# A planned instruction order: ties to VectorE, engines of early pieces as a list, the verdict before the last down projection

## The chip, the cores and the metric

The kernel runs on one core of one Trainium2 chip. The metric is the time of one execution in microseconds (us). TensorE multiplies matrices, VectorE, ScalarE and GpSimd work on tiles, SP issues all transfers.

## The reference

A linear attention with decay over 768 steps, for 4 batches and 8 heads of 48 features, and behind it a feed-forward layer with the maximum of three projections. Cut to what is computed:

```
for t in range(S):                       # 768 steps, per batch and head
    cur = outer(u * k[t], v[t])
    y[t] = r[t] @ (state + cur)
    state = w * state + outer(k[t], v[t])
x = y over all heads                     # 3072 tokens x 384
h = max(x @ w1, x @ w2, x @ w3)          # 3072 x 768
out = h @ w_out                          # 3072 x 384
```

## The kernel before, in words

The 768 steps are cut into 12 chunks c of 64 steps (`NCH`, `C`); a chunk holds 256 tokens (4 batches). Heads go in two halves q of four. For each (c, q) the features of k and r are scaled by powers of the decay (`scale`, line 526), TensorE forms scores, a mask keeps what lies before the diagonal (line 628), the bonus u comes onto the diagonal, and TensorE forms the values from the scores and the carried state (`values`, line 661). The state is brought forward by one product per chunk (`keys`, `into_state`, line 649).

Numbers are split in a high and a low fp16 part, and three of the four products are taken. In chunks 0 and 1 (`FULL`) the attention runs in fp32 instead; there the state is spread into its operand by `state_apart` (line 676), four ScalarE instructions, and the bonus comes as a product pp of the scaled k and r (`joined`, line 561), a matmul `bonus` with it (line 569), and a predicated copy. From `EARLY` on the bonus is formed from the token layout.

`ffn(c)` (line 1090) takes six blocks f of the hidden layer. For each, three up projections go into accumulators of a ring of four (`psm`, line 720); the first becomes m by `first` on ScalarE (line 735), the other two by `least` on VectorE, a maximum (line 739). ScalarE makes the high part hh (line 742), GpSimd or VectorE the low part hl (`lows_by` and `h_low`, lines 744 to 748). Three down projections m = 0, 1, 2 then leave through ScalarE (line 765) and SP (line 1128). The weights come as 64-bit words in 16 pieces of 576 KB; each piece takes ScalarE (line 377), VectorE (line 381), ScalarE (line 384) and VectorE again (line 388) to split.

The fast path is exact only while the inputs lie in ranges. So sums of squares are taken on the way (lines 392, 514), `check_ends` (line 778) and `check` (line 782) test them on VectorE, `count` (line 794) adds up the good rows on TensorE, `verdict` (line 798) makes a flag, and `flagged` (line 804) loads it into a register of every engine. Line 1180 branches on it: with a flag of 0 the general path behind it is jumped over.

What sets the order: every engine's queue is written out by a planner. `do` (line 166) records a piece of work with a due number, engine, cost, what it reads and writes, and the buffers that it takes. The due number grows with the chunk, and `SHIFT` adds a number by engine, kind and one of four stages. `order` (line 190) then lists the pieces one by one: among those that could start first by the planner's clock it takes the lowest due number. `near` marks pieces of VectorE and GpSimd that read two operands from SBUF; the planner doesn't let one of each engine overlap. When a VectorE piece of that kind is about to be listed and a GpSimd one could start as early, both compete by their due numbers. The listed order is emitted at lines 1175 to 1177, each queue runs it strictly in turn, and semaphores hold what isn't ready.

Of the kernel before, what the change touches and what calls it, by code (L numbers as in the profile page):

```python
# [1 line left out]

# [18 lines left out]
C = 64  # L21
# [5 lines left out]
U = 8  # L27
# [44 lines left out]
class Plan:  # L72

    LAG = {"pe": 0.22, "dve": 0.12, "act": 0.15, "pool": 0.12, "sp": 0}
    FREE = dict(pe=5.1, dve=4.4, act=4.0, pool=10.5, sp=2.1)
    SLACK = dict(pe=0.022, dve=0, act=0, pool=0, sp=0.324)
    LANES, BEFORE, BEHIND = 8, 1.1, 0.9
    PHASE, PIPE, STIR = -0.626, 3.4, 1.1
    RATE = {"feat": 300e3, "tok": 280e3, "word": 325e3, "again": 280e3, "u": 300e3, "kb": 200e3, "ktb": 235e3, "sb": 265e3, "vb": 255e3, "io": 300e3, "vl": 240e3, "x4": 150e3}
    STAGES = (-0.01, 1.6, 4.2)  # L80
    SHIFT = {
        "act ah": (-51.918, -65.498, -45.263, -70.501),
        "act eye16": (2.479, 10.868, 2.479, 2.479),
        "act hh": (-33.526, -14.287, -83.034, -18.026),
        "act his": (-38.269, -57.533, -17.347, -17.347),
        "act io": (-20.889, -66.792, 14.503, -29.26),
        "act kdh": (-43.057, -58.602, -10.774, -29.53),
        "act kt": (-30.9, -10.226, 7.514, 7.514),
        "act ktdh": (-3.857, 40.692, 1.455, 33.711),
        "act ktdl": (3.565, -0.867, 3.565, 3.565),  # L90
        "act m": (-70.203, -41.092, -60.922, -75.724),
        "act rh": (19.916, 12.704, 32.612, 53.416),
        "act sb": (0.145, -0.176, -10.989, -10.989),
        "act sdh": (-16.606, -58.921, 1.393, -19.385),
        "act sq": (-1.212, -23.443, 14.89, -12.959),
        "act state": (33.684, 26.281, 28.467, 28.467),
        "act tkf": (-17.604, -31.369, -17.604, -17.604),
        "act tkt": (22.733, 36.039, 22.733, 22.733),
        "act u": (4.631, 27.167, 4.631, 4.631),
        "act vdh": (-17.326, -39.923, -45.144, -6.375),  # L100
        "act wsq": (10.215, 10.215, 10.215, -8.248),
        "act xh": (30.286, 24.252, -17.669, -20.556),
        "act xsq": (-6.009, -27.049, 24.787, 11.067),
        "act ztop": (-4.699, -20.204, 10.624, 10.624),
        "dve a": (26.38, 26.38, 11.139, -1.961),
        "dve al": (17.989, 15.173, 12.796, 3.439),
        "dve am": (55.107, 70.564, 45.761, 45.639),
        "dve ama": (30.643, 9.956, 13.112, 13.112),
        "dve ends": (12.35, 12.35, 12.35, -28.973),
        "dve flag": (1.454, 1.454, 1.454, -27.608),  # L110
        "dve good": (-5.938, -5.938, -5.938, -17.176),
        "dve hl": (-37.322, -78.745, -108.013, -56.219),
        "dve kT": (-16.831, -12.831, -12.831, -12.831),
        "dve kdl": (0.885, -7.723, -39.713, -26.204),
        "dve ktdl": (-5.025, -5.025, -36.996, 18.823),
        "dve lo": (-0.26, -6.619, 7.806, 7.806),
        "dve m": (-20.646, -47.146, 3.792, -49.546),
        "dve pp": (9.143, -7.503, -7.503, -7.503),
        "dve rT": (10.984, 17.021, 17.021, 17.021),
        "dve rl": (-7.775, 1.143, 7.87, 0.054),  # L120
        "dve sdl": (10.363, 27.381, 7.967, -24.341),
        "dve state": (-21.286, 12.093, -11.87, 12.772),
        "dve uw": (0.32, 1.8, 1.8, 1.8),
        "dve vdl": (-17.961, -18.008, 30.606, -24.481),
        "dve wc": (-6.358, 8.855, 8.855, 8.855),
        "dve word": (-0.926, 1.508, 3.967, 3.967),
        "dve xl": (-27.474, -19.943, -51.504, -89.07),
        "pe bo": (-52.734, 1.414, 10.831, 10.831),
        "pe count": (3.343, 3.343, 3.343, 38.72),
        "pe dn": (-0.067, -15.416, -14.654, -0.182),  # L130
        "pe ke": (-0.01, -23.579, -0.382, 0.04),
        "pe kea": (-7.875, 12.914, 2.838, 2.838),
        "pe read": (4.637, 4.637, 4.637, 18.248),
        "pe sc": (-0.084, -31.697, -0.512, -0.419),
        "pe sca": (-3.935, 71.214, 12.28, 12.28),
        "pe th": (-9.587, -62.178, -9.587, -9.587),
        "pe tha": (23.917, 65.739, 34.635, 34.635),
        "pe turned": (-13.591, 14.048, -13.591, -13.591),
        "pe up": (-0.117, -7.456, -0.433, -0.157),
        "pe va": (-0.206, 16.327, -15.548, -0.297),  # L140
        "pe vaa": (-12.853, -16.75, -19.32, -19.32),
        "pool am": (-17.715, -17.715, -5.033, -19.033),
        "pool hl": (-48.799, -21.273, -76.69, -49.446),
        "pool kT": (34.361, 53.386, 38.392, 59.601),
        "pool kdec": (-10.665, -10.665, 19.908, 1.651),
        "pool pp": (27.125, 25.693, 41.112, 41.112),
        "pool rT": (43.765, 63.373, 35.752, -3.803),
        "sp again": (8.471, 8.471, 8.471, 55.836),
        "sp feat": (-52.564, 4.808, 0.643, 1.927),
        "sp first": (-13.276, -15.501, -15.501, -15.501),  # L150
        "sp io": (14.829, -21.632, 41.797, 39.859),
        "sp kb": (-2.952, -16.917, 3.534, 14.738),
        "sp ktb": (17.782, -6.916, 9.699, 12.373),
        "sp sb": (-23.628, -37.745, -29.113, 17.159),
        "sp tok": (-33.778, 55.686, -34.574, -42.289),
        "sp u": (-34.129, -15.755, -34.129, -34.129),
        "sp vb": (7.415, 6.46, 39.433, -0.198),
        "sp vl": (-12.349, 18.562, 18.562, 18.562),
        "sp word": (-15.193, 28.55, -3.374, -3.374),
# [6 lines left out]
    def do(self, due, eng, cost, fn, reads=(), writes=(), takes=(), size=0, near=0, n=1, active=1.0, kind=None):  # L166
# [4 lines left out]
        name = eng + " " + what  # L171
# [15 lines left out]
        self.todo.append(dict(n=k, due=due, due0=due0, stage=stage, eng=eng, cost=cost, fn=fn, need=need, takes=takes, size=size, near=near, nd=n, active=active, kind=name,  # L187
                              rate=self.RATE[what] if size else 0, touch={*reads, *writes, *new}))

    def order(self):  # L190
# [16 lines left out]
        def earliest(p):  # L207
# [1032 lines left out]
```

## Time and profile before

| | |
|---|---|
| runs, us | 385.55, 385.65, 388.21; median 385.65 |
| the profiled execution | 389.68 us, span 387.9 us |
| TensorE matmul busy | 372.6 us, 96% of the span, 5039 |
| VectorE busy | 252.4 us, 65%, 519 |
| ScalarE busy | 256.5 us, 66%, 673 |
| GpSimd busy | 185.3 us, 48%, 194 |
| DMA | 78.28 MB, mean 202 GB/s |
[...]

Times in the rows count from the start of the span. PE is TensorE, PEld its weight loads, DVE VectorE, ACT ScalarE, POOL GpSimd; a q behind the name is the engine's sequencer, which also handles semaphores, register loads and branches. A busy time holds a wait for operands that begins after an instruction has started. Idle time is given with what ended it. [...]

### The profile page before, as it was taken

The numbers are of one execution on the slowest core, as the hardware profiler recorded it, in microseconds if no ns is written. First come the engines' busy times: TensorE is split into PE (matmuls) and PEld (weight loads), VectorE is DVE, ScalarE is ACT, GpSimd is POOL, SyncE is SP. The second block draws the span as 40 slices with busy tenths as digits, with TensorE's granted clock in tenths as the row PEclk, the third lists the DMA queues.
The fourth block names the chain that finished last, engine by engine and source line by source line (L and its number), as shares of the span: only waits on it lengthen the run. The fifth ranks groups of instructions, "written<-read, shape, count | busy, mean of one in ns | idle before, by whom it ended". The sixth has DMA issues, their size and how long they took to land.

```text
span 387.9 us, 12500 instructions
## 1 busy us (share of the span) xinstructions
PE 372.6 (96%) x5039; PEld 333.3 (86%) x5039; DVE 252.4 (65%) x519; ACT 256.5 (66%) x673; POOL 185.3 (48%) x194
## 2 busy tenths in 40 slices
PE   8978999999999999979999999999999999999993
PEld 5857888999999999959999999999999989999883
DVE  6678999958586675967585585485586385352530
ACT  2968788576856846736766766666766787994421
POOL 9561442555855853844735745745745614020210
PEclk9989999999999999989999999999999999999997
DMA  7994499689966996972886886886896885930001
GB/s 195 377 294 147 131 349 275 190 234 248 298 164 189 269 252 181 286 222 80 226 226 177 245 227 170 253 228 159 265 229 179 238 233 139 284 119 29 16 0 48
DMA packets 32320, 78.28 MB, mean 202 GB/s; under 512 B 8576, under 2 KB 13824, under 8 KB 32256
## 3 DMA queue, kind: packets, MB, share of 16 engines
q1 hardware_dynamic: 32256, 77.42, 69.8%
q8 instruction: 41, 0.67, 0.7%
q14 instruction: 23, 0.19, 0.2%
HBM read 37.59 MB, written 4.72 MB: 109 GB/s over the span
## 4 chain that ended last, share of the span: by engine, by line
PE 69%; DMA 12%; DVE 5%; ACT 4%; issue 3%; POOL 3%; SPq 2%; DVEq 0%; ACTq 0%; POOLq 0%
PE psm L720 56%; DMA tok<-in_tok_dram 8%; PE psa L674 6%; PE psa L614 4%; DMA feat<-in_feat_dram 2%; ACT junk L514 1%; DMA kb<-kd 1%; DMA sb<-sd 1%; DVE m L739 1%; DVE sd L694 1%; PE psa L575 1%; PE psa L586 1%; POOL pp L564 1%; ACT kd L498 1%; DVE xl L715 1%
## 5 line engine op out<-in xcount | busy, mean ns | idle before, releaser
L720 PEld LDWEIGHTS <-w 128*128 128x128 f16 x2592 | 250.2, 98 | 34.0 <-issue 4.6
L720 PE MATMUL psm<-xh,w 128*128 128x256 f16 x1296 | 222.3, 274 | 3.2 <-DVE m L739 3.2
L720 PE MATMUL psm<-xl,w 128*128 128x256 f16 x648 | 154.7, 274 | 0.0
L739 DVE SCALAR_TENSOR_TENSOR m<-psm,m 128x256 f32<-128x256 f32 x144 | 60.4, 421 | 65.3 <-PE psm L720 43.1
L748 POOL TENSOR_TENSOR hl<-m,hh 128x256 f16<-128x256 f32 x55 | 39.3, 715 | 98.7 <-ACT hh L742 94.1
L529 POOL TENSOR_TENSOR feat<-feat,wrt 128x512 f32<-128x512 f32 x44 | 58.0, 1327 | 31.3 <-DMA feat<-in_feat_dram 31.3
L720 PE MATMUL psm<-hh,w 128*128 128x256 f16 x432 | 56.0, 273 | 0.0
L742 ACT CAST hh<-m 128x256 f16<-128x256 f32 x72 | 28.5, 398 | 36.3 <-DVE m L739 36.0
L514 ACT ACTIVATE junk<-tok 128x384 bf16<-128x384 f32 x72 | 37.5, 521 | 18.1 <-DMA tok<-in_tok_dram 17.2
L548 POOL TENSOR_TENSOR am<-tok,u_sb 128x384 f32<-128x384 f32 x18 | 19.6, 1087 | 54.7 <-DVE al L638 44.3
L715 DVE SCALAR_TENSOR_TENSOR xl<-psa,xh 32x256 f16<-32x256 f32 (+2 forms) x60 | 28.3, 472 | 16.2 <-ACT xh L710 15.4
L735 ACT ACTIVATE m<-psm 128x256 f32<-128x256 f32 x72 | 27.2, 377 | 10.4 <-PE psm L720 9.2
L720 PE MATMUL psm<-hl,w 128*128 128x256 f16 x216 | 33.4, 273 | 0.0
L710 ACT ACTIVATE xh<-psa 32x256 f16<-32x256 f32 (+2 forms) x60 | 24.9, 415 | 9.3 <-PE psa L674 8.9
L674 PE MATMUL psa<-rh,sb 128*128 128x64 f16 x320 | 29.5, 193 | 0.0
L674 PE MATMUL psa<-ah,vb 128*128 128x64 f16 x320 | 29.5, 193 | 0.0
L674 PE MATMUL psa<-rl,sb 128*128 128x64 f16 x160 | 28.4, 193 | 0.0
L674 PE MATMUL psa<-al,vb 128*128 128x64 f16 x160 | 28.4, 193 | 0.0
L765 ACT ACTIVATE io<-psm 128x256 f32<-128x256 f32 x36 | 13.0, 374 | 21.5 <-PE psm L720 21.4
L674 PEld LDWEIGHTS <-vb 128*128 128x128 f16 x480 | 26.3, 98 | 0.4
L674 PEld LDWEIGHTS <-sb 128*128 128x128 f16 x480 | 25.0, 98 | 0.0
L503 DVE TENSOR_TENSOR kd<-feat,kd 128x512 f16<-128x512 f32 x20 | 19.0, 952 | 4.4 <-ACT kd L498 4.3
(107 smaller groups left out, 546.8 us busy)
## 6 DMA issues: line engine op xcount, KB each, us to landing
tok<-in_tok_dram SPq DMA_DIRECT2D x24, 576.0 KB, 6.8
feat<-in_feat_dram SPq DMA_DIRECT2D x22, 512.0 KB, 5.2
raw<-in_ws_dram SPq DMA_DIRECT2D x12, 576.0 KB, 6.8
kb<-kd SPq DMA_DIRECT2D x20, 256.0 KB, 5.4
kb<-kd SPq DMA_DIRECT2D x20, 248.0 KB, 5.5
ktb<-ktd SPq DMA_DIRECT2D x18, 256.0 KB, 7.2
out_dram<-io SPq DMA_DIRECT2D x36, 128.0 KB, 4.9
ktb<-ktd SPq DMA_DIRECT2D x18, 248.0 KB, 7.5
```

The costliest lines, as they stand in the source:

```text
L503: nc.vector.tensor_tensor(out=dense.dense[:, 1, :, 0:w], in0=src, in1=dense.dense[:, 0, :, 0:w], op=ALU.subtract)
L514: nc.scalar.activation(out=junk[:, 0:U * D].rearrange("p (u d) -> p u d", u=U), in_=src, func=AF.Square, scale=scale, accum_out=stat[:, ki ...
L529: (nc.gpsimd if c else nc.vector).tensor_tensor(out=t[n], in0=t[n], in1=tb, op=ALU.mult)
L548: helper(c).tensor_tensor(out=w.rearrange("p (g b) d -> p g b d", g=2), in0=t["r"], in1=by_token(u_sb, q), op=ALU.mult)
L674: nc.tensor.matmul(out=t["va"][0:n, i, :], lhsT=a, rhs=b, start=k == 0, stop=k == len(prods) - 1)
L710: nc.scalar.mul(out=hi, in_=src, mul=x_scale(c))
L715: nc.vector.scalar_tensor_tensor(out=lo, in0=src, scalar=x_scale(c), in1=hi, op0=ALU.mult, op1=ALU.subtract)
L720: nc.tensor.matmul(out=ps, lhsT=a, rhs=b, start=first and n == 0, stop=last and n == len(prods) - 1)
L735: nc.scalar.mul(out=m, in_=ps, mul=by)
L739: nc.vector.scalar_tensor_tensor(out=m, in0=ps, scalar=by, in1=m, op0=ALU.mult, op1=ALU.max)
L742: nc.scalar.copy(out=h[0][:, f, :], in_=m)
L748: lows_by(c, f).tensor_tensor(out=h[1][:, f, :], in0=m, in1=h[0][:, f, :], op=ALU.subtract)
```

## The change

*The planner.* All numbers of `SHIFT` are new (a few are shown), as are `FREE` (when each engine is first free) and `SLACK` (how far a piece may be put off for one with a lower due number). A `near` piece of GpSimd is taken to start `SEIZE` = 0.33 us later. In a tie it is now the GpSimd piece that can be displaced, by any VectorE piece that could start as early. Costs of some pieces are longer.

*Engines.* `flex` records a piece with several engines, and `CHOICE` names, by the piece's number in the order of recording, which of them is taken; a piece without an entry takes the first. The first engine of the list is VectorE for scaling (chunks 0 to 3), pp and, in chunks 0 and 1, hl; it is ScalarE for m, the first state and its spread.

*The checks.* The check of the ends moves from due 4.9 to 10, behind the start of chunk 9 instead of chunk 4. The check of the sums, the count, the flag and its load are recorded before `ffn` of the last chunk, and its last down projection (m = 2) now reads "read", so that it is listed behind the load. The last sum of squares of x and the repeated sums of the weights fall due earlier. The conditional general path stays at the end.

```diff
-    FREE = dict(pe=5.1, dve=4.4, act=4.0, pool=10.5, sp=2.1)
-    SLACK = dict(pe=0.022, dve=0, act=0, pool=0, sp=0.324)
+    FREE = dict(pe=5.15, dve=4.2, act=4.2, pool=10.5, sp=2.36)
+    SLACK = dict(pe=0, dve=0.059, act=0.146, pool=0.589, sp=0.419)
+    SEIZE = 0.33
...
+    CHOICE = {30: 1, 31: 2, 47: 1, 134: 1, 135: 1, 137: 1, 152: 1, 153: 1, 178: 1, 186: 1, 188: 1, 196: 1, 202: 1, 212: 1, 234: 1, 235: 1, 241: 1, 264: 1, 265: 1, 296: 1, 302: 1, 310: 1, 312: 1, 318: 1, 320: 1, 326: 1, 334: 1, 336: 1, 342: 1, 359: 1, 391: 1, 392: 1}
     SHIFT = {
...
-        "dve word": (-0.926, 1.508, 3.967, 3.967),
+        "dve word": (88.415, 131.798, 76.497, 30.189),
-        "pe up": (-0.117, -7.456, -0.433, -0.157),
+        "pe up": (-44.638, -143.074, -77.684, -76.534),
-        "pe read": (4.637, 4.637, 4.637, 18.248),
+        "pe read": (0, 0, 0, -80.672),
-        "sp feat": (-52.564, 4.808, 0.643, 1.927),
+        "sp feat": (-27.4, -40.095, 30.336, -8.959),
-        "sp vl": (-12.349, 18.562, 18.562, 18.562),
+        "sp vl": (-17.172, -10.657, -10.657, -0.468),
-        "sp word": (-15.193, 28.55, -3.374, -3.374),
+        "sp word": (68.802, 88.992, 63.732, 36.065),
...
+        if alts:
+            eng, cost, near = (base, *alts)[self.CHOICE.get(k, 0)]
+            fn = partial(fn, eng)
...
             elif p["eng"] == "pool" and p["near"]:
+                t += self.SEIZE
...
-            if e == "dve" and self.todo[n]["near"]:
-                rival = [m for m in when if self.todo[m]["eng"] == "pool" and self.todo[m]["near"] and when[m] <= when[n] + 1e-6]
+            if e == "pool" and self.todo[n]["near"]:
+                rival = [m for m in when if self.todo[m]["eng"] == "dve" and when[m] <= when[n] + 1e-6]
...
-    def state_apart(q):
-        for g in range(2):
-            j = 2 * q + g
-            for hh in range(2):
-                w = sb[q].wide[HS[hh], g * B:(g + 1) * B, hh * D:(hh + 1) * D]
-                nc.scalar.mul(out=w, in_=state[HS[hh], j], mul=wc[HS[hh], j:j + 1])
+    def state_apart(q, e):
+        for hh in range(2):
+            if e != "act":
+                w = sb[q].wide[HS[hh], :, hh * D:(hh + 1) * D].rearrange("p (g b) d -> p g b d", g=2)
+                by = wc[HS[hh], 2 * q:2 * q + 2].unsqueeze(2).unsqueeze(3).broadcast_to([C, 2, B, D])
+                by_name[e].tensor_tensor(out=w, in0=state[HS[hh], 2 * q:2 * q + 2], in1=by, op=ALU.mult)
+                continue
+            for g in range(2):
+                j = 2 * q + g
+                nc.scalar.mul(out=sb[q].wide[HS[hh], g * B:(g + 1) * B, hh * D:(hh + 1) * D], in_=state[HS[hh], j], mul=wc[HS[hh], j:j + 1])
 
...
+    def flex(due, options, fn, **on):
+        fn = fn if len(options) > 1 else partial(fn, options[0][0])
+        do(due, *options[0][:2], fn, near=options[0][2], alts=options[1:], **on)
...
+        options = [("dve", dve(U * C), 1), ("pool", 1.27, 1)] if c < 4 else [("pool", 1.27, 1)]
...
+            flex(due - 0.32 + 0.02 * i, options, lambda e, n=n: scale(c, q, n, e), reads=reads, writes=[(n, c, q)])
+            flex(due - 0.16, [("dve", dve(U * C), 1), ("pool", 1.27, 1)], lambda e: joined(c, q, e), reads=[f, ("kT", c, q), ("rT", c, q)], takes=[("pp", ("pp", c, q))])
+            flex(due + 0.02, [("act", act(U * D), 0), ("dve", 0.5, 0)], lambda e: into_state(c, q, e), reads=[("ke", c, q)], writes=[s])
+            flex(due + 0.06, [("act", 1.85, 0), ("pool", 2.1, 1), ("dve", 0.95, 1)], lambda e: state_apart(q, e), reads=[s, "wc"], writes=[("sb", q)])
...
+                    flex(due - 0.2, [("act", act(TOK), 0), ("dve", dve(TOK), 0)][:2 if c < 2 else 1], lambda e, f=f: do_tile(("m", c, f), first(T["up", c, f, 0], TOK, H16, e)), reads=[("up", c, f, 0)], writes=[] if f else [("begun", c)], takes=[("m", ("m", c, f))])
+            options = [("dve", dve(TOK), 1), ("pool", 0.73, 1)]
+            if c > 1:
+                options = options[1:] if f < NF - 1 else options[:1]
+            flex(due - 0.1, options, lo, reads=[m, ("hh", c, f), *([("hl", c)] if f else [])], writes=[("hl", c, f)], takes=[] if f else [("hl", ("hl", c))])
...
+            reads = (["read"] if c == NCH - 1 and m == NM - 1 else []) + [k for a in ("hh", "hl") for k in ((a, c), *((a, c, f) for f in fs))] + [(a, *n) for n in w for a in ("his", "lo")]
...
-        ffn(c)
+            ffn(c)
     for n in range(NW):
         for h in range(2):
-            again(n, h, NCH - 2.6 + 0.25 * n + 0.12 * h)
+            again(n, h, NCH - 2.8 + 0.22 * n + 0.11 * h)
     for i in range(2 * EARLY):
         squares_again(i // 2, i % 2, NCH - 3 + 0.25 * i)
-    do(4.9, "dve", 1.2, check_ends, reads=[("begun", 4)], writes=["ends"])
-    do(NCH - 0.4, "dve", 1.5, check, reads=["ends", *(k for k in plan.wrote if k[0] in ("sq", "xsq", "wsq"))], writes=["good"])
-    do(NCH - 0.35, "pe", 0.1, count, reads=["good"], takes=[("psa", "count")])
-    do(NCH - 0.35, "dve", 0.1, verdict, reads=["count"], writes=["flag"])
-    do(NCH - 0.16, "pe", 0.1, flagged, reads=["flag"], writes=["read"])
+    do(NCH - 2, "dve", 2.4, check_ends, reads=[("begun", NCH - 3)], writes=["ends"])
+    do(NCH - 1 + 0.45, "dve", 2.4, check, reads=["ends", *(k for k in plan.wrote if k[0] in ("sq", "xsq", "wsq"))], writes=["good"])
+    do(NCH - 1 + 0.5, "pe", 0.1, count, reads=["good"], takes=[("psa", "count")])
+    do(NCH - 1 + 0.5, "dve", 0.15, verdict, reads=["count"], writes=["flag"])
+    do(NCH - 1 + 0.55, "pe", 0.1, flagged, reads=["flag"], writes=["read"])
+    ffn(NCH - 1)
```

## Rows read from the trace of the kernel before

**Rows 1.** Stretch, length; busy (x) of PE, PEld, DVE, ACT, POOL; granted clock, DMA.

```profile
28.00:76.00 48.00, 46.56 (x603) 40.95 (x602) 44.32 (x76) 38.02 (x81) 17.78 (x15) 1.00 0.70 213
200.00:250.00 50.00, 50.00 (x710) 45.78 (x708) 29.21 (x62) 32.04 (x88) 31.20 (x32) 1.00 0.79 220
300.00:340.00 40.00, 39.36 (x540) 35.78 (x538) 21.58 (x48) 33.23 (x97) 13.11 (x14) 1.00 0.80 226
```

**Rows 2.** TensorE's waits over the span: us in total, times, longest.

```profile
PE psm L720 <- DVE m L739: 3.2, 2, 2.5
PE psa L575 <- POOL pp L564: 2.6, 1, 2.6
PE psa L674 <- issue: 1.3, 1, 1.3
```

**Rows 3.** Busy time and granted clock in the stretches behind TensorE's waits.

```profile
22.00:24.00 2.00, 1.32 (x6) 0.76 (x8) 2.00 (x3) 1.20 (x3) 0.63 (x1) 0.54 1.02 229
24.00:26.00 2.00, 2.00 (x13) 1.10 (x10) 0.58 (x1) 0.00 (x0) 0.01 (x1) 0.60 0.97 323
168.00:170.00 2.00, 2.00 (x14) 1.62 (x14) 1.95 (x5) 1.35 (x3) 0.38 (x1) 0.73 0.97 227
170.00:172.00 2.00, 2.00 (x12) 1.39 (x11) 0.29 (x1) 1.17 (x4) 1.92 (x3) 0.50 1.02 399
```

**Rows 4.** GpSimd in order of time: start us, us, what.

```profile
18.95 3.68 POOL L564 TENSOR_TENSOR pp<-feat 128x512 f32<-128x512 f32 x1
...
162.00 2.92 POOL L529 TENSOR_TENSOR feat<-feat,wrt 128x512 f32<-128x512 f32 x2
```

**Rows 5.** VectorE in order of time, near two of TensorE's waits.

```profile
31.55 0.73 DVE L628 COPY_PREDICATED am<-cs,psa 128x512 f32<-128x512 int32 x1
...
151.80 0.74 DVE L694 SCALAR_TENSOR_TENSOR sd<-state,wc,sd 128x192 f16<-128x192 f32 x2
...
154.47 0.16 DVE L772 TENSOR_SCALAR bt<-wu_sb 128x4 f32<-128x4 f32 x1
...
156.77 0.16 DVE L774 TENSOR_TENSOR ends<-ends,bt 128x4 f32<-128x4 f32 x1
...
162.38 2.77 DVE L694 SCALAR_TENSOR_TENSOR sd<-state,wc,sd 128x192 f16<-128x192 f32 x2
```

**Rows 6.** Instructions by line and shape: count, busy us, mean ns, idle before.

```profile
L739 DVE SCALAR_TENSOR_TENSOR m<-psm,m 128x256 f32<-128x256 f32 x144 | 60.4, 421 | 65.3 <-PE psm L720 43.1 <-ACT m L735 14.7 <-ACT kd L498 3.2
...
L748 POOL TENSOR_TENSOR hl<-m,hh 128x256 f16<-128x256 f32 x55 | 39.3, 715 | 98.7 <-ACT hh L742 94.1 <-DVE am L628 2.5 <-DMA out_dram<-io 1.8
...
L564 POOL TENSOR_TENSOR pp<-feat 128x512 f32<-128x512 f32 x4 | 7.9, 1975 | 0.3
...
L681 ACT ACTIVATE sb<-state,wc 64x192 f32<-64x192 f32 x8 | 3.6, 452 | 0.2
...
L564 DVE TENSOR_TENSOR pp<-feat 128x512 f32<-128x512 f32 x2 | 1.4, 692 | 0.1
```

**Rows 7.** The end in order of time: ScalarE's last copy, SP's last transfer.

```profile
381.70 0.38 ACT L765 ACTIVATE io<-psm 128x256 f32<-128x256 f32 x1 [1.58 <-PE psm L720]
...
382.60 0.34 SPq L1128 DMA_DIRECT2D out_dram<-io  x1
```

**Rows 8.** Lines 805, 1180, 1235: duration ns least, median, longest; first and last start.

```profile
L805 ACTq TENSOR_LOAD <-flag x1: 463/463/463, 382.0 to 382.0; - x1
L805 PEldq TENSOR_LOAD <-flag x1: 491/491/491, 382.0 to 382.0; - x1
...
L1180 PEldq COMPARE_BRANCH  x1: 4198/4198/4198, 382.6 to 382.6; - x1
...
L1235 SPq EVENT_SEMAPHORE  x14: 17/28/567, 385.8 to 387.9; - x14
```

**Rows 9.** DMA issues from 370 us on: KB each, us to landing.

```profile
out_dram<-io SPq DMA_DIRECT2D x3, 128.0 KB, 1.8
```

**Rows 10.** VectorE near the end: the check's last instruction.

```profile
364.40 0.28 DVE L792 TENSOR_REDUCE good<-ok 128x1 f32<-128x125 f32 x1
```

More of the change, by code (lines that the diff above doesn't have):

```diff
@@ L1 @@
 from contextlib import ExitStack
+from functools import partial
 import concourse.bass as bass
@@ L86 @@
[L86 to L125, printed above, removed]
@@ new lines @@
+        "dve ama": (-67.852, -74.779, -10.739, 0.799),
+        "dve ends": (0, 0, 0, -22.298),
+        "dve flag": (0, 0, 0, 58.918),
+        "dve good": (0, 0, 0, -31.946),
+        "dve hl": (23.491, -32.082, -106.608, -65.147),
+        "dve kT": (-85.346, -11.836, 20.754, -9.76),
+        "dve kdl": (22.717, 51.739, -58.583, 17.126),
+        "dve ktdl": (-31.022, -31.022, -11.392, -41.137),
+        "dve lo": (-1.191, 40.138, -21.062, -19.786),
+        "dve m": (-101.783, -139.093, 24.699, 46.278),
@@ L164, in __init__, with do @@
         self.bufs, self.todo, self.wrote, self.read, self.turn = bufs, [], {}, {}, {}
-    def do(self, due, eng, cost, fn, reads=(), writes=(), takes=(), size=0, near=0, n=1, active=1.0, kind=None):
+    def do(self, due, eng, cost, fn, reads=(), writes=(), takes=(), size=0, near=0, n=1, active=1.0, kind=None, alts=()):
         k = len(self.todo)
@@ L170, in do @@
         what = kind or (made if isinstance(made, str) else made[0])
-        name = eng + " " + what
+        name, base = eng + " " + what, (eng, cost, near)
+        if alts:
+            eng, cost, near = (base, *alts)[self.CHOICE.get(k, 0)]
+            fn = partial(fn, eng)
         stage = sum(due > s for s in self.STAGES)
@@ L186, in do @@
         need.discard(k)
-        self.todo.append(dict(n=k, due=due, due0=due0, stage=stage, eng=eng, cost=cost, fn=fn, need=need, takes=takes, size=size, near=near, nd=n, active=active, kind=name,
+        self.todo.append(dict(n=k, base=base, alts=alts, due=due, due0=due0, stage=stage, eng=eng, cost=cost, fn=fn, need=need, takes=takes, size=size, near=near, nd=n, active=active, kind=name,
                               rate=self.RATE[what] if size else 0, touch={*reads, *writes, *new}))
@@ L647, in keys, with into_state @@
             three(t["ke"][:, i, :], [ktb.on[s][i] for s in range(2)], [vd[q].dense[:, s, i, 0:D] for s in range(2)], True, True)
-    def into_state(c, q):
+    def into_state(c, q, e="dve"):
         ps = raws[c, q].pop("ke")
         if c == 0:
-            nc.scalar.copy(out=units(state[:, 2 * q:2 * q + 2]), in_=ps)
+            (nc.scalar.copy if e == "act" else nc.vector.tensor_copy)(out=units(state[:, 2 * q:2 * q + 2]), in_=ps)
             return
@@ L731, in up, with first @@
         return ps
-    def first(ps, n, by):
+    def first(ps, n, by, e):
         m = tmp.tile([P, n], F32, name="m", bufs=3)
-        nc.scalar.mul(out=m, in_=ps, mul=by)
+        if e == "act":
+            nc.scalar.mul(out=m, in_=ps, mul=by)
+        else:
+            nc.vector.tensor_scalar(out=m, in0=ps, scalar1=by, scalar2=None, op0=ALU.mult)
         return m
@@ L908 @@
     do_tile = T.__setitem__
+    by_name = dict(dve=nc.vector, pool=nc.gpsimd, act=nc.scalar)
+    def flex(due, options, fn, **on):
+        fn = fn if len(options) > 1 else partial(fn, options[0][0])
+        do(due, *options[0][:2], fn, near=options[0][2], alts=options[1:], **on)
     def dma(due, fn, size, n=1, **on):
-        do(due, "sp", 0.42 * n, fn, size=size, n=n, **on)
+        do(due, "sp", (0.64 if on.get("kind") == "vl" else 0.42) * n, fn, size=size, n=n, **on)
     def helping(c, columns):
@@ L959, in scaled @@
     def scaled(c, q, due):
[L960 removed]
+        options = [("dve", dve(U * C), 1), ("pool", 1.27, 1)] if c < 4 else [("pool", 1.27, 1)]
         f = ("feat", c, q)
[L962 to L963 removed]
+        for i, (n, reads) in enumerate((("kT", [f]), ("rT", [f, ("rraw", c, q)]))):
+            flex(due - 0.32 + 0.02 * i, options, lambda e, n=n: scale(c, q, n, e), reads=reads, writes=[(n, c, q)])
     def before_scores(c, q, due):
@@ L975, in before_mask @@
         if c < EARLY:
-            do(due - 0.16, *(("pool", 1.28) if c else ("dve", dve(U * C))), lambda: joined(c, q), reads=[f, ("kT", c, q), ("rT", c, q)], takes=[("pp", ("pp", c, q))], near=int(c > 0))
+            flex(due - 0.16, [("dve", dve(U * C), 1), ("pool", 1.27, 1)], lambda e: joined(c, q, e), reads=[f, ("kT", c, q), ("rT", c, q)], takes=[("pp", ("pp", c, q))])
             do(due - 0.12, "pe", 0.9, lambda: bonus(c, q), reads=[("pp", c, q), "uw"], takes=[("psa", ("bo", c, q))])
```

125 lines of the change are left out of this document (71 added, 54 removed).

## The prediction

> **What bounds the kernel now.** I read the busy time by stage first, then the waits of TensorE, then the clock in the stretches behind its waits, then VectorE and GpSimd in those stretches, last the chain behind the last matmul.
>
> By stage, TensorE is busy all 50.00 us of 200 to 250 us, at full clock [rows 1]. There no reordering can gain: the work is the same before and after. VectorE is the engine to watch early: 44.32 of 48.00 us between 28 and 76 us, against 29.21 of 50.00 and 21.58 of 40.00 us in the two later stretches [rows 1].
>
> TensorE's waits are few [rows 2]: 2.6 us for the product pp, 1.3 us put down to issue, and 3.2 us in two waits for m (2.5 and so 0.7 us). Behind the long ones the clock falls to its lower level. From 22 to 24 us the granted clock is 0.54 over 1.32 us of matmul, from 24 to 26 us 0.60 over 2.00 us, which costs 1.32 x 0.46 + 2.00 x 0.40 = 1.4 us. From 168 to 172 us it costs 2.00 x 0.27 + 2.00 x 0.50 = 1.5 us [rows 3]. So there are **early holes** of 2.6 + 1.3 + 1.4 = 5.3 us and a **middle hole** of 2.5 + 1.5 = 4.0 us.
>
> Each has its cause. pp of 128x512 took 3.68 us on GpSimd from 18.95 us [rows 4], against 0.69 us of the same form on VectorE [rows 6]. VectorE was running weight conversions meanwhile, and pp came last. The wait of 1.3 us ends with the mask, which VectorE did at 31.55 us for 0.73 us [rows 5]: the values matmul that follows it starts at once. The middle hole begins where the check of the ends takes VectorE from 154.47 to 156.93 us, six instructions on 4 columns [rows 5]. Then two state instructions, 2.77 us for a pair, stand beside 2.92 us of scaling on GpSimd from 162.00 us [rows 4, 5], and m is late.
>
> **The sum's base.** The profiled execution took 389.68 us, 387.90 of them span and 1.78 around it. The runs shown have a median of 385.65, 4.03 less, just about the middle hole. I read this as: the hole belongs to some executions and not to the median one. So the sum goes 389.68 - 4.0 (middle hole) = 385.7, and from there.
>
> **The change, part by part.**
>
> 1. *Order.* Every due time is shifted anew, GpSimd's shared operations are listed 0.33 us later, VectorE wins a tie, some costs are longer. This adds no instruction and removes none, so it is worth only what it does to holes: at best +5.3 us for the early ones, all closed. At worst it makes others; no row shows the new order, so the lower end is one more hole of the middle kind, -4.0. I take **3.0**. The wait for pp needs other work in TensorE's order, or an earlier pp. At half the pair of scalings of the same form, 1.46 us [rows 4], pp would end at 20.4 instead of 22.6 us, so 2.2 of its 2.6 us and, with a hole that short, the 1.4 us of clock are to be had: 3.6. The wait of 1.3 us may stay or go, half is 0.65. Against these 4.25 I set 1.25 for a new small hole of the second kind, since VectorE gets fuller (next). On SP the new shifts still rank the first features and values before the weight words, so the first transfers keep their order; what the later ones do has no row and lies within the two ends.
>
> 2. *Engines chosen.* Counting the calls in the order in which they are listed, the 32 numbers come out so. To VectorE: seven first maxima m from ScalarE (three of chunk 0, four of chunk 1), pp of (1,1) and (2,1) and the scaling of k in (3,0) from GpSimd, the first state of pair half 0 and its spread into sb, now two instructions instead of four. To GpSimd: four low parts hl (f = 0, 1, 3 of chunk 0 and f = 5 of chunk 1), and sb of half 1, in two instructions. Everything else flexible stays where it was. For VectorE that is 7 x 0.42 = 2.9 us of m, 3 x 0.69 = 2.1 of products and scaling, less 4 x 0.42 of hl, about as one m [rows 6]: +3.3 us, most of it between 28 and 76 us, where it has 48.00 - 44.32 = 3.7 us idle [rows 1]. The state and its spread lie before that; two instructions of 0.5 to 0.7 us each by the nearest VectorE rows and one copy, +1.9. ScalarE loses 8 x 0.452 = 3.6 us of sb [rows 6]. GpSimd gains 4 x 0.715 = 2.9 us of hl and loses two pp and a scaling at 1.46 to 1.98 us [rows 4, 6]: nearly even. On the path I cost this at **0**, covered by the 3.7 us idle; if that cover is gone, m is late next, and with it the ring of four accumulators that TensorE fills.
>
> 3. *Check of the ends*, from about chunk 5 to chunk 10: 2.46 us of VectorE [rows 5] go to a stretch with 40.00 - 21.58 idle [rows 1]. **0** there. In the middle it takes away one of the two causes of that hole, already in the base.
>
> 4. *Verdict earlier.* Now the count of the good rows, the flag and its load into a register lie behind the last matmul. The last copy starts at 381.70 us [rows 7], TensorE's load of the flag at 382.0 for 0.49 us, its branch at 382.6, and the branch takes 4.2 us, to 386.8; the last semaphore is at 387.9 [rows 8]. With the load taken earlier, the branch can start as the last matmul is issued: 382.6 - 381.7 = 0.9 us earlier. More, if the sequencer runs ahead of the matmuls; then the end is set by the output instead: copy 0.38 us [rows 7], issue 0.34 [rows 7], landing 1.8 [rows 9], and 387.9 - 386.8 = 1.1 of closing barriers give 381.70 + 3.6 = 385.3, which is 2.6 earlier. The other end: the load stands in all five queues at the place of the read, TensorE pays up to 0.49 us between matmuls, VectorE's last m and hl, ScalarE's copies and SP's output transfers queue behind theirs, and 0.9 - 0.5 = 0.4 is left. I take **1.2**, nearer to the lower pair of rows. The verdict must be in hand by then: the check's last instruction ran at 364.40 us [rows 10], 17 us before the end, and its input, the last sum of squares of x, is listed earlier; **0**.
>
> [...] No row here shows how far the sequencer runs ahead.
>
> Sum: 385.7 - 3.0 - 1.2 = 381.5, against the median 385.65 - 4.2 = 381.45. I say **381.4**.
>
> **The rivals.**
>
> *A, the holes only move.* The new order closes the wait for pp and opens waits of the same size elsewhere before 80 us; the tail is all that stays: 385.65 - 1.2 = 384.4. For it: the order is made from listed costs, and in the trace the same form takes 0.69 alone, 1.98 us on GpSimd in the mean and 3.68 at worst [rows 4, 6], so small errors decide. Against it: the two costliest waits have a named cause that other work can fill.
>
> *B, slower: VectorE becomes the bound between 28 and 76 us.* Its 3.7 us idle shrink to 0.4 by the 3.3 us of part 2. From then on each instruction that has to wait for GpSimd comes straight out of TensorE: the state pair took 0.74 us at 151.80 us and 2.77 us at 162.38 us [rows 5], 2.0 us of it waiting. Two such collisions make 4.0 us, less 0.4, and each hole of that kind has its fall of the clock, 1.5 us: 3.6 + 3.0 = 6.6. With the tail's 1.2 and without the early gain 385.65 + 6.6 - 1.2 = 391.1. It decides from the point at which VectorE has no idle slice between 28 and 76 us. For it: 92% busy there now. Against it: three products leave GpSimd, so there is less to collide with.
>
> *C, the branch under the last matmuls.* The sequencer reaches the branch while matmuls still run, the output sets the end: 381.4 - 1.4 = 380.0. For it: ScalarE's load of the flag stands at the same 382.0 us although its copy runs until 382.08 [rows 7, 8]. [...]
>
> *D, the verdict is late or the read blocks the queues*, so TensorE stands before the last down projection: the load's 0.5 us, and up to 1.2 us for the rest of the tail's gain: 381.4 + 1.7 = 383.1. Against it: 17 us of slack.
>
> **How the numbers follow.** Chances: forecast 0.46, A 0.24, B 0.14, C 0.10, D 0.06. The forecast's own range is 379.3 to 383.5: 3.0 give or take 1.5 and the tail from 0.6 to 1.8. The range on record goes down to C with the early holes closed further, 378.5, and up past A with a further 2.1 us of new holes, 386.5; B lies outside. Faster by over 1%, what a measurement of this kernel can tell from no change, is under 381.8: 0.6 of the forecast (0.28), nearly all of C (0.10), a quarter of A and D (0.07), in sum 0.45. Slower is over 389.5: most of B, 0.13. The rest is 0.42.
>
> **What would show it.** Right: no wait of TensorE for pp over 1 us, no granted clock under 0.9 between 16 and 32 us, no TensorE idle near 164 us; the load of the flag stands before the last down projection and the branch at most 0.2 us after the last matmul. A: as much idle time of TensorE before 80 us as now, behind other releasers. B: VectorE over 47 of 48 us between 28 and 76 us, and m as releaser of TensorE's waits there. C: a branch that starts before the last matmul ends. D: a wait of TensorE on the flag. I am wrong if the waits close and the time stays, or if the branch takes much more or less than 4.2 us.

## The result, and the profile after

In the first comparison, four executions of each, the kernel took **381.71 us** after the change (379.99 to 381.82) and 386.53 before: ratio 0.986, 95% interval 0.981 to 0.991. Run again later beside other kernels (twelve executions, 35 of before) it took 382.21 against 385.97: ratio 0.992, 0.988 to 0.995. Ratios leave out slow executions, medians and spreads hold them all. So it is 0.8% to 1.4% faster, 3.2 to 5.4 us. The profiled execution after took 381.82 us, 380.3 of them span.

By stage, with the columns of [rows 1]:

```profile
22.00:24.00 2.00, 1.55 (x15) 1.28 (x14) 1.97 (x4) 2.00 (x5) 1.24 (x2) 1.00 1.03 337
24.00:26.00 2.00, 2.00 (x23) 1.88 (x21) 1.96 (x5) 2.00 (x5) 0.00 (x0) 1.00 1.17 256
28.00:76.00 48.00, 45.90 (x566) 40.40 (x564) 46.09 (x83) 32.46 (x70) 24.05 (x18) 1.00 0.69 218
150.00:200.00 50.00, 50.00 (x692) 45.64 (x691) 36.79 (x67) 31.15 (x88) 35.68 (x32) 1.00 0.76 214
200.00:250.00 50.00, 49.84 (x675) 45.40 (x672) 41.69 (x73) 34.13 (x93) 32.47 (x30) 1.00 0.86 227
```

The granted clock, as a share of the full one, is 1.00 where it was 0.54 and 0.60 [rows 3], and TensorE has no idle time from 150 to 200 us: the middle hole is gone. But from 28 to 76 us TensorE works 45.90 us where it worked 46.56 [rows 1], and VectorE has 1.9 us idle where it had 3.7. TensorE's waits (us in total, times, longest), answering to [rows 2]; "issue" is a wait that nothing in the profile explains:

```profile
PE psm L728 <- ACT m L744: 1.7, 1, 1.7
PE psa L590 <- issue: 1.0, 1, 1.0
PE psm L728 <- DVE m L750: 0.8, 2, 0.6
...
PE psa L579 <- DVE pp L571: 0.2, 1, 0.2
```

The wait for pp fell from 2.6 to 0.2 us; a wait of 1.7 us for ScalarE's m is new. Its cause is on VectorE and ScalarE, in order of time:

```profile
23.83 0.74 DVE L388 SCALAR_TENSOR_TENSOR raw<-raw,ztop 128x576 int32<-128x576 int32 x1
...
28.38 1.82 DVE L388 SCALAR_TENSOR_TENSOR raw<-raw,ztop 128x576 int32<-128x576 int32 x1
```
```profile
30.23 0.73 ACT L391 ACTIVATE w<-raw 128x576 f16<-128x576 f32 x1 [2.76 <-DVE raw L388]
30.87 1.52 ACT L718 ACTIVATE xh<-psa 96x256 f16<-96x256 f32 x4
32.41 0.84 ACT L384 CAST ztop<-raw 128x576 f16<-128x576 bf16 x1
33.27 0.38 ACT L744 ACTIVATE m<-psm 128x256 f32<-128x256 f32 x1
```

VectorE's word (L388 here), a step of splitting a weight piece, took 0.74 us at 23.83 and 1.82 at 28.38, beside GpSimd's scaling (26.33 to 29.58 us); ScalarE stood 2.76 us for it, and the m that TensorE wanted came three pieces later in ScalarE's queue.

The end, answering to [rows 7, 8]: the start of TensorE's first down projection of the last piece, its last down projection, ScalarE's last copy, and then the lines of the load (L813), the branch (L1197) and the closing semaphores (L1252), each with its least, median and longest ns and its starts:

```profile
371.12 1.26 PE L728 MATMUL psm<-hh,w 128*128 128x256 f16 x10
...
375.06 1.47 PE L728 MATMUL psm<-hh,w 128*128 128x256 f16 x12
376.37 0.82 PE L728 MATMUL psm<-hl,w 128*128 128x256 f16 x6
```
```profile
377.22 0.38 ACT L773 ACTIVATE io<-psm 128x256 f32<-128x256 f32 x1 [1.58 <-PE psm L728]
```
```profile
L813 PEldq TENSOR_LOAD <-flag x1: 491/491/491, 371.6 to 371.6; - x1
...
L1197 POOLq EVENT_SEMAPHORE  x4: 17/43/43, 374.8 to 377.1; - x4
L1197 POOLq COMPARE_BRANCH  x1: 45/45/45, 372.2 to 372.2; - x1
L1197 DVEq COMPARE_BRANCH  x1: 72/72/72, 372.6 to 372.6; - x1
L1197 PEldq COMPARE_BRANCH  x1: 3798/3798/3798, 375.1 to 375.1; - x1
...
L1252 SPq EVENT_SEMAPHORE  x14: 17/28/28, 378.5 to 380.2; - x14
```

TensorE's branch (PEldq) starts at 375.1 us, as the last 18 matmuls begin, and is over at 378.9. From the start of the last copy to the end of the span it is 380.3 - 377.2 = **3.1 us**, where it was 387.9 - 381.7 = 6.2 [rows 7, 8]. I call this length the tail from here on.

### The profile page after: what moved, and what is told of

Read it like the earlier page. It is cut to its first block, busy times and chain, and to the rows that moved or that the text cites. A ratio compares the mean times of both kernels' runs of the same rounds, so it can differ in the third digit from the quotient of the medians.

```text
span 380.3 us, 12517 instructions
## 1 busy us (share of the span) xinstructions
PE 370.3 (97%) x5039; PEld 332.8 (88%) x5039; DVE 276.9 (73%) x528; ACT 250.2 (66%) x657; POOL 201.4 (53%) x197
## 4 chain that ended last, share of the span: by engine, by line
PE 74%; DVE 7%; DMA 7%; ACT 4%; issue 3%; POOL 2%; SPq 2%; DVEq 0%; ACTq 0%; POOLq 0%
PE psm L728 61%; PE psa L678 6%; PE psa L618 5%; DMA feat<-in_feat_dram 2%; DMA kb<-kd 2%; DVE raw L388 1%; PE psa L590 1%; DMA raw<-in_ws_dram 1%; DVE xl L723 1%; ACT xh L718 1%; DMA vb<-vd 1%; DVE m L750 1%; ACT junk L521 1%; PE psa L579 1%; DVE w L395 1%
## 5 line engine op out<-in xcount | busy, mean ns | idle before, releaser
L728 PE MATMUL psm<-xh,w 128*128 128x256 f16 x1296 | 215.8, 273 | 3.1 <-ACT m L744 1.7
L756 POOL TENSOR_TENSOR hl<-m,hh 128x256 f16<-128x256 f32 x59 | 42.9, 733 | 71.8 <-ACT hh L753 71.6
L536 POOL TENSOR_TENSOR feat<-feat,wrt 128x512 f32<-128x512 f32 x43 | 65.1, 1525 | 20.3 <-DMA feat<-in_feat_dram 20.3
L555 POOL TENSOR_TENSOR am<-tok,u_sb 128x384 f32<-128x384 f32 x18 | 20.4, 1132 | 59.8 <-DVE al L642 57.6
L702 DVE SCALAR_TENSOR_TENSOR sd<-state,wc,sd 128x192 f16<-128x192 f32 x36 | 28.6, 834 | 3.7 <-ACT sd L695 3.7
L744 ACT ACTIVATE m<-psm 128x256 f32<-128x256 f32 x65 | 24.6, 378 | 8.3 <-PE psm L728 5.2
L564 POOL TENSOR_TENSOR am<-cs,a 128x512 f32<-128x512 f32 x18 | 22.6, 1255 | 3.3 <-DVE a L560 3.2
```

Of the source, the lines that this page charges most:

```text
L536: by_name[e].tensor_tensor(out=t[n], in0=t[n], in1=tb, op=ALU.mult)
L564: helper(c).tensor_tensor(out=t["a"], in0=eye.unsqueeze(1).broadcast_to([P, U, C]), in1=t.pop("sum").unsqueeze(2).broadcast_to([P, U, C]), ...
L702: nc.vector.scalar_tensor_tensor(out=sd[q].dense[:, 1, us, 0:D], in0=state[:, j], scalar=by[:, j:j + 1], in1=sd[q].dense[:, 0, us, 0:D], o ...
L728: nc.tensor.matmul(out=ps, lhsT=a, rhs=b, start=first and n == 0, stop=last and n == len(prods) - 1)
L744: nc.scalar.mul(out=m, in_=ps, mul=by)
L756: by_name[e].tensor_tensor(out=h[1][:, f, :], in0=m, in1=h[0][:, f, :], op=ALU.subtract)
```

## The experiments

They ran in three groups, with the kernel before in each: medians 387.08, 385.97 and 386.48 us over 29, 35 and 35 executions, scattered over 8 to 10 us. Ratios are to the kernel before of the same group, with 95% intervals; where two ratios of different groups are compared, the text says so.

**One part alone, or one part undone.** First the verdict alone, in before:

```diff
 order = plan.order()
+late = [p for p in order if p["kind"] in ("pe count", "dve flag", "pe read")]
+order = [p for p in order if p not in late]
+i = max(j for j, p in enumerate(order) if p["kind"] == "pe dn")
+order[i:i] = late
```

> The kernel before with one move: count, flag and its load stand directly before the last down projection. Theory (the branch runs under the last matmuls): TensorE's branch starts about 2 us before the last matmul ends, the span ends 3.1 us after the last matmul instead of 6.2, the time falls by 3.0 us, ratio to before 0.992. Rival (the branch waits for the last matmul and only the flag leaves the tail): the branch starts as the matmuls end, the gain is 0.9 to 1.2 us, ratio 0.997.

0.998 (0.994 to 1.002). TensorE in order of time at the end, and its branch:

```profile
378.81 0.19 PE L796 MATMUL psa<-good,ones 128*1 128x1 f32 x2
379.74 1.47 PE L720 MATMUL psm<-hh,w 128*128 128x256 f16 x12 [0.74 <-DVE flag L800]
```
```profile
L1184 PEldq COMPARE_BRANCH  x1: 3898/3898/3898, 379.8 to 379.8; - x1
```

The branch lies under the last matmuls and the tail is 385.2 - 381.9 = 3.3 us. But count, flag and load stand in one chain here, and TensorE waits 0.74 us for the flag. The mechanism is the theory's, but the ratio, 0.8 us, does not show the 2 us that are left; this run alone would leave the question open.

Next the check of the ends, late instead of early, in before:

```diff
+moved = [p for p in order if p["kind"] == "dve ends"]
+order = [p for p in order if p not in moved]
+i = next(j for j, p in enumerate(order) if p["kind"] == "dve good")
+order[i:i] = moved
```

> The kernel before with one move: the check of the ends stands just before the check of the sums instead of in chunk 5. Theory (those 2.5 us of VectorE make the middle hole): no wait of TensorE over 1 us between 150 and 180 us, granted clock 1.00 there; executions of before that have the hole are 4 us longer, those without it the same, so the ratio lies between 0.990 and 1.000. Rival (GpSimd's scaling beside the state pair makes it alone): the wait of 2.5 us near 165 us stays in the profile.

0.995 (0.990 to 1.000). The stretch of the middle hole in this kernel (first row) and in the kernel of the third group that moves pp and the verdict and keeps the check where before had it (second row):

```profile
150.00:200.00 50.00, 50.00 (x683) 45.66 (x681) 36.17 (x71) 32.73 (x89) 30.92 (x32) 1.00 0.84 233
```
```profile
150.00:200.00 50.00, 48.40 (x658) 44.08 (x656) 39.08 (x76) 31.68 (x88) 28.66 (x29) 1.00 0.81 224
```

All six profiles of kernels with the check early have the wait for m there (2.5 us in before, 1.6 in the five others); this one and the changed kernel have none. This kernel's profile also has, by chance, next to nothing of the early hole: TensorE waited 0.2 us for pp. GpSimd's product pp, VectorE's word that starts beside it, and the same word in before:

```profile
19.77 1.27 POOL L564 TENSOR_TENSOR pp<-feat 128x512 f32<-128x512 f32 x1
```
```profile
20.39 1.28 DVE L381 SCALAR_TENSOR_TENSOR raw<-raw,ztop 128x576 int32<-128x576 int32 x1
```
```profile
19.41 0.75 DVE L381 SCALAR_TENSOR_TENSOR raw<-raw,ztop 128x576 int32<-128x576 int32 x1
```

The scaling ahead of pp could begin at 16.92 us, when the features had landed, instead of 15.84. Then pp took 1.27 us instead of 3.68 [rows 4], and VectorE's word 1.28 instead of 0.75. The queues of both engines are the same there; between these two executions, which of the two instructions takes longer goes with when a transfer lands. The order of the starts doesn't tell which it is: GpSimd's record starts 0.62 us ahead of VectorE's word here (19.77 and 20.39) and 0.46 us ahead in before (18.95 and 19.41). What the longer one waits for, no view shows.

Now the changed kernel with its verdict read last again:

```diff
+late = [p for p in order if p["kind"] in ("pe count", "dve flag", "pe read")]
+order = [p for p in order if p not in late] + late
```

> The changed kernel with count, flag and load put back behind the last matmul. Theory (branch under the matmuls): 381.7 + 3.1 = 384.8 us, tail 6.2 us again. Rival (only 0.9 to 1.2 us come from the tail, the rest from the order): 382.9 us.

1.005 (1.001 to 1.008), a median of 387.11 us: slower than before, and over the theory's 384.8. Against the changed kernel's 0.992 of the second group that is 1.3%, 5.0 us, for three pieces at another place. The tail of its profile is 384.4 - 376.7 = 7.7 us:

```profile
L1199 POOLq EVENT_SEMAPHORE  x4: 17/43/43, 380.3 to 382.6; - x4
L1199 PEldq COMPARE_BRANCH  x1: 4222/4222/4222, 377.6 to 377.6; - x1
```

It is 1.5 us longer than in before. Here GpSimd's four semaphores behind the branch come last, at 382.6 us, behind the end of TensorE's branch at 381.8; they are 2.3 us apart, as in the changed kernel, where that is hidden, and 0.2 us in before.

And the new queues with the 17 pieces whose engine changed on their former ones:

```diff
+FORMER = {30: "act", 31: "act", 47: "act", 155: "pool", 271: "pool", 358: "pool", ...}
...
-fn = partial(fn, eng)
+fn = partial(fn, self.FORMER.get(k, eng))
```

> The changed kernel, every queue in the order of its list, but the 17 pieces that changed engine run on their former one. Theory (order and engines go together): TensorE's waits before 80 us grow by 2 to 4 us, 384 to 386 us. Rival 1 (the order alone gives the early gain): within 0.7 us of 381.7. Rival 2 (VectorE is the bound from 16 to 76 us, and taking 5 us from it helps): 380.5 us or less.

1.012 (1.007 to 1.018), a median of 389.81 us, over the theory's 384 to 386. TensorE's waits (am are the masked scores):

```profile
PE psm L730 <- DVE m L752: 3.3, 4, 1.6
PE psa L592 <- DVE am L634: 2.8, 1, 2.8
PE psm L730 <- ACT m L746: 1.8, 1, 1.8
```

**Second group.** The changed kernel as it is:

> The changed kernel itself, run again beside the three below, as the level that they are held against. Theory list (the new queues take away the holes before 80 us and make the kernel's executions less dependent on how VectorE and GpSimd meet): 0.986 of before, as in the first comparison, and a scatter of its executions well below the 8 us of before. Rival luck (the 4 us were drawn from the scatter of before): 0.993 to 1.000 of before, with executions scattered as widely as before's.

0.992 (0.988 to 0.995): over the first comparison's 0.986, and not apart from the rival's 0.993. The executions lie from 380.13 to 388.42 us, as wide as before's, so it isn't a steadier kernel: part of the first comparison's gain may have been the draw. Then before's queues with the new engines:

```diff
+NOW = {155: "dve", 271: "dve", 358: "dve", 30: "dve", 31: "dve", 47: "pool", ...}
-joins(c).tensor_tensor(out=t["pp"], ...)
+now(joins(c)).tensor_tensor(out=t["pp"], ...)
...
```

> The queues of before, in before's order, with the 17 pieces on the engines that the change chose; the verdict where it was. Theory of the prediction (the choice by itself is worth nothing): 0.997 to 1.003 of before. Rival (VectorE, given 3.3 us more between 28 and 76 us with 3.7 us idle in the kernel before, becomes the bound there while the order isn't fitted to it): 1.004 to 1.010 of before, with TensorE waiting for VectorE's m or low parts for over 2 us. Rival (the choice carries the gain): 0.990 or less.

1.008 (1.005 to 1.012): 3.2 us slower, the first rival. TensorE's waits:

```profile
PE psa L580 <- POOL pp L569: 2.5, 1, 2.5
PE psm L731 <- DVE m L753: 2.5, 3, 1.6
PE psa L679 <- DVE al L643: 1.4, 2, 1.0
```

The early hole is as in before, and the middle hole is there (1.6 of the 2.5). The wait for al, the low part of the masked scores, does not come from the new engines: 1.0 us of it stands in the first run of this section too. The next one adds the verdict's move of the first diff, so it lacks only the order:

> The queues of before with the new engines and with the verdict's count, flag and load in front of the last down projection: all of the change but the order of the queues, so what lies between this and the changed kernel is the order. Theory list: 0.996 to 1.003 of before, so the order is worth 1.0% to 1.7%, of which part lies in the early read itself: in the order of before the flag stands unhidden before the last down projection (0.7 us of TensorE's wait when the read alone was moved), in the new one VectorE has its last check done 16 us ahead. Rival (the read and the engines are the gain, the order adds nothing): 0.986 to 0.990.

1.005 (1.001 to 1.009), just over the theory's 1.003. TensorE waits 0.7 us for the flag, as in the first run. From the run before it to this one, 0.3%, or 1.4 us, is the verdict. From here to the changed kernel, 1.3%, is the order, within queues that have the new engines; that order has the moved check of the ends in it, and the count further ahead.

Then nine moves by hand in the changed kernel's queues; (39, 45) puts piece 39 ahead of piece 45 in its engine's queue, and `plan_order` is the order of the changed kernel:

```diff
+order = relisted(plan, plan_order, [(39, 45), (40, 59), (46, 56), (41, 60), (180, 76), (182, 77), (184, 143), (188, 143), (155, 143)])
```

> The changed kernel with nine pieces moved by hand in its queues before 76 us: on TensorE the values of half 1 ahead of its keys; on ScalarE the high part of half 1's x ahead of the top of z, its state ahead of a weight's split, and one m ahead of another; on VectorE the low part of half 1's x ahead of a word, and three later pieces and one pp ahead of low parts that nobody waits for yet. Theory order (what is left of TensorE's idle time before 76 us, 1.7 us behind ScalarE's m, 1.0 behind keys and 1.3 at the start of the stretch, is a matter of who comes first): 1 to 3 us under the changed kernel, 0.992 to 0.997 of it. Rival bound (VectorE works 11.6 of 12 us from 16 us on and 46.1 of 48 us from 28 to 76 us, so TensorE waits elsewhere for the same time): within 0.3% of the changed kernel, the waits under other names.

0.995 (0.993 to 0.998), 0.3% over the changed kernel. By stage:

```profile
28.00:36.00 8.00, 8.00 (x133) 6.90 (x132) 7.83 (x15) 4.77 (x11) 2.39 (x3) 1.00 0.75 256
36.00:52.00 16.00, 13.96 (x192) 12.26 (x187) 15.90 (x23) 12.89 (x24) 7.27 (x6) 1.00 0.61 214
```

The hole that the moves aimed at is closed, 8.00 of 8.00 where the changed kernel has 6.09. The next stretch loses 2.04 of 16.00, where the changed kernel loses nothing, and VectorE is busy 15.90 of those 16. That is as the rival, VectorE as the bound, has it; the last run of this section asks the same from the other side. For the changed kernel itself the stretches from 16 to 76 us are

```profile
16.00:28.00 12.00, 10.61 (x149) 9.34 (x150) 11.63 (x16) 9.02 (x16) 6.99 (x7) 1.00 1.06 324
28.00:36.00 8.00, 6.09 (x55) 5.08 (x53) 7.53 (x13) 4.47 (x9) 2.96 (x3) 1.00 0.82 288
36.00:52.00 16.00, 16.00 (x268) 14.90 (x269) 15.05 (x27) 12.91 (x23) 9.06 (x6) 1.00 0.67 232
52.00:76.00 24.00, 23.81 (x245) 20.41 (x244) 23.51 (x45) 15.08 (x39) 12.03 (x11) 1.00 0.65 186
```

so VectorE is busy 57.72 of 60 us there, TensorE 56.51.

**Third group.** In before, the one product pp of piece 1, half 0 on VectorE, and its place in the list moved to fit:

```diff
-joins(c).tensor_tensor(out=t["pp"], ...)
+(nc.vector if (c, q) == (1, 0) else joins(c)).tensor_tensor(out=t["pp"], ...)
...
+p = next(p for p in order if p["n"] == 137)
+order.remove(p)
+order.insert(next(i for i, o in enumerate(order) if o["n"] == 52), p)
```

> The kernel before with one thing changed: the product pp of piece 1, half 0, which GpSimd made (3.68 us in the profiled execution of before, 1.27 where VectorE was not at it), is made by VectorE, between its word (1,0) and its low part (0,0). Theory collision (the early hole comes of GpSimd waiting on VectorE over the operands in SBUF): TensorE's wait for pp of 2.5 us falls below 1, the cold clock between 16 and 28 us goes, and the kernel takes 0.990 to 0.995 of before. Rival A of the prediction (holes only move: the low parts behind the product on VectorE are 0.7 us later): 0.997 to 1.003, the waits under other names.

1.000 (0.996 to 1.004): the early hole's clearest cause is gone and the time is the same. TensorE's waits:

```profile
PE psm L720 <- DVE m L739: 2.2, 2, 1.6
...
PE psa L575 <- DVE pp L564: 1.2, 1, 1.2
PE psa L674 <- DVE al L638: 1.2, 1, 1.2
PE psa L614 <- issue: 1.0, 2, 0.6
```

pp cost 1.2 us and not 2.6, and the clock stays at 1.00 up to the last matmul. Of 16 to 76 us TensorE is idle for 1.5 in this profile, of 76 to 150 us for 2.2; in before's it was 4.35 and nothing. So the holes may have moved. But al, the largest wait after 76 us, stands with 1.0 us in the first run of this section too, where pp was left alone. And a second reading fits as well: most executions of before may never have had the early hole in full. The first run has before's queues up to its end, and its profile has the hole with its lower clock, 0.86 over 16 to 28 us, which takes 12 x 0.14 = 1.7 us, 0.4% of the span, out of its mean clock of 0.994; nine of its twelve executions have a mean clock of 0.997 or more, which has no room for that. This run doesn't part the two readings.

With the verdict's move added, this time with the count ahead of the last up projection and the load behind the first down projection:

```diff
+late = [p for p in order if p["kind"] in ("pe count", "dve flag", "pe read")]
+order = [p for p in order if p not in late]
+for p, k in zip(late, (1548, 1549, 1553)):
+    order.insert(next(i for i, o in enumerate(order) if o["n"] == k), p)
```

> The kernel before with the product pp on VectorE as in the run beside it, and with the verdict's count in front of the last up projection, its flag in VectorE's queue there, and its load between the first and the second down projection of the last piece, so that the flag is there before it is asked for. All else, queues and engines, as before. Theory tail (TensorE's branch of 4.2 us runs under the last matmuls, 2.9 us less from the last copy to the end) with theory collision: 2.9 + 2 us under before, 0.985 to 0.990, level with the changed kernel. Rival (the gain of the changed kernel is its new list as a whole): 0.993 to 1.000.

0.993 (0.989 to 0.997): over the theory's 0.990, since the 2 us for pp did not come, but not apart from the changed kernel's 0.992 of the second group. The one difference to the run beside it is the verdict: 0.7%, 2.6 us, by the two intervals some 2 us either way. Its tail:

```profile
379.69 0.38 ACT L765 ACTIVATE io<-psm 128x256 f32<-128x256 f32 x1 [1.58 <-PE psm L720]
```
```profile
L1187 PEldq COMPARE_BRANCH  x1: 3918/3918/3918, 377.5 to 377.5; - x1
```

382.9 - 379.7 = 3.2 us, with no wait for the flag. At last two tries at a better kernel, from the changed one: one move, and three moves with three m back on ScalarE.

```diff
+order = relisted(plan, plan_order, [(180, 76)])
```

> The changed kernel with one of the nine moves alone: ScalarE's m of piece 0, block 1 ahead of the split of weight (2,1), for which ScalarE stood 2.76 us; TensorE waited 1.7 us for that m. Theory order: 0.5 to 1.7 us under the changed kernel, so 0.987 to 0.990 of before. Rival bound (VectorE works 57.7 of the 60 us from 16 to 76 us, so the hole moves behind its m): 0.990 to 0.994, with TensorE's wait for VectorE's m grown by as much.

0.993 (0.989 to 0.997), as the changed kernel in the second group and as the rival has it, with the hole under another name:

```profile
PE psm L759 <- DVE m L781: 2.6, 3, 1.7
```

```diff
-fn = partial(fn, eng)
+fn = partial(fn, "act" if k in (188, 196, 212) else eng)
...
+order = relisted(plan, plan_order, [(180, 76), (182, 143), (184, 143)])
```

> The changed kernel with three moves (ScalarE's m of the run beside it, and VectorE's two m of the same block ahead of the low part of piece 1's x), and three of the m that the change gave to VectorE between 33 and 50 us back on ScalarE, 1.2 us of VectorE's work. Theory bound (VectorE sets the time before 76 us): the relief pays where the moves alone did not, 1 to 2 us under the changed kernel, 0.986 to 0.989 of before. Rival (ScalarE comes too late with these m, since each then stands behind a weight's split): 0.993 or more, with TensorE waiting for ScalarE's m.

0.997 (0.994 to 1.000): not better either. TensorE's waits:

```profile
PE psm L759 <- DVE m L781: 2.4, 3, 1.2
PE psm L759 <- ACT m L775: 2.0, 2, 1.8
```

The time is the rival's, but its cause is not seen: the long wait for ScalarE's m, 1.8 us, lies between 150 and 200 us, far from the three m, and before 80 us TensorE still waits mostly for VectorE. Taking 1.2 us off VectorE did not make it less busy: it shows 58.68 of the 60 us from 16 to 76 us, in 98 instructions, against 57.72 in 101 in the changed kernel. Its busy time is not a measure of its work: the same word takes 0.74 or 1.82 us in the changed kernel. Whether VectorE's load is the bound there stays open.

## Why the prediction was right in its sum and wrong in its terms

The forecast, 381.4 us, met the median of 381.71, but by luck: its 4.2 us were split as 3.0 for the order and 1.2 for the verdict, and the runs put most of it on the verdict, 3.1 us by the ends of the profiles, and 0.1 to 2.3 us on all the rest. The two errors cancelled.

- **The base.** "The hole belongs to some executions and not to the median one" was said of the wrong hole. The middle hole's wait is in all six profiles of kernels that check the ends early, 1.6 us of it with the clock at 1.00; what only before's profile has are the 0.9 us more and the 1.5 us of lower clock, 2.4 of its 4.0 us. The early hole with its lower clock, which the sum left in the base, is missing in at least nine of twelve executions of the first run. Before's profiled execution was a bad one: no other of before's 99 has a mean clock under its 0.986, and their median is 0.996.
- **Part 1, the order, taken at 3.0.** Between the two profiles the wait for pp fell by 2.4 us and the lower clock went, as forecast. The step that failed is to take these 3.6 us off a median whose executions, by the clocks of the first run, mostly don't have them in full. What the forecast set against them, 1.25 for a new small hole, was too little, too: TensorE works 45.90 us between 28 and 76 us, less than the 46.56 of before. Of the 60 us from 16 to 76, TensorE was idle 4.35 in before's profile, 3.49 and 2.25 in the two of the changed kernel. From 16 to 370 us it was 7.5, then 4.5 and 3.6, but before's execution was a bad one. Over many executions, the gain of 3.2 to 5.4 us less the tail's 3.1 leaves **0.1 to 2.3** for order, engines and the check together. That is nearer to rival A, "the holes only move". The runs with one and with nine moves show holes that do: in both, a hole that is closed opens behind another of VectorE's instructions. That VectorE's load is the reason is not shown.
- **Part 2, the engines, taken at 0.** Shown wrong as a number that stands by itself: in the old queues the new engines cost 0.8%, in the new queues the former engines cost 2.1% (1.012 against 0.992, across two groups). Engines and order fit each other, and only the pair has a price. Rival B's condition, VectorE over 47 of 48 us, did not come about: it was 46.09.
- **Part 3, the check of the ends, taken at 0.** In the profiles its removal from 154 us closes the middle hole: 1.6 us of TensorE's wait, 1.8 us by the ratio of the run that moved it alone, with an interval that just reaches 0.
- **Part 4, the verdict, taken at 1.2.** The tail fell from 6.2 to 3.1 us, which is 2.6 us by the ratios of the two runs that differ only in this. The other pairs give 0.8 and 1.4 us, both with 0.7 us of wait for the flag, and 5.0 us, 1.5 of it GpSimd's semaphores; each is uncertain by some 2 us. The step that failed is "the branch can start as the last matmul is issued": it starts as the last 18 begin, which is rival C. The load cost TensorE nothing: it ran at 371.6 us beside matmuls that follow each other from 371.12 to 377.19. The upper bound of 2.6 was too low, too: copy, issue, landing and barriers, summed to 3.6 us behind the start of the last copy, took 3.1. Rival D's wait did show, 0.7 us, in the two runs where count and load stood directly behind each other; in the changed kernel the 15 matmuls of the first down projection lie between.

In the changed kernel the branch lies under the last down projection: its 18 matmuls begin at 375.06 us, the branch at 375.1. In all nine profiles with the early load it begins within 0.2 us of the start of that projection, also where TensorE had stood 0.74 us for the flag just before; so the 18 is the size of that projection, and no run here shows how far TensorE's sequencer runs ahead of its matmuls or what holds the branch until then.

What stays open: how the 0.1 to 2.3 us divide between order, engines and check (the runs that undo one part give more than the whole, as if each half was fitted to the other), and why GpSimd's semaphores behind the branch lie 2.3 us apart in some kernels.

## What to carry to other kernels

When the last thing of a kernel is a branch on a value, have the value and its load well ahead of the last matmuls: here three pieces brought 2.6 us, give or take 2, and all the rest of the change 0.1 to 2.3. A hole of TensorE behind one named instruction is worth its length only if the executions that are timed have it, and if no other opens behind it: nine moves won 1.9 us in one stretch and lost 2.0 in the next. And don't explain the difference between one profiled execution and the median by the hole that happens to be as long: look whether the hole is in other profiles of the same queues, and whether the mean clock of the other executions has room for it.

## What the hardware showed that was not expected

TensorE's branch over the skipped path took 3.76 to 4.30 us in all fourteen profiles, alone or under matmuls, against 45 and 72 ns for the same instruction on GpSimd and VectorE. And one kernel, with nothing changed, took 382.43 to 390.73 us in 35 executions; one place where executions part, in two profiles whose queues are the same there, is the product pp: 3.68 us where the features had landed at 15.84 us, 1.27 where they had at 16.92.
